# Splitting the scalar steps of a weight conversion, moving one state scaling, and taking two more diagonals from token rows

## The chip, the cores and the metric

The kernel runs on one core of one Trainium2 chip. A core has TensorE (PE, with its weight loads PEld), VectorE (DVE), ScalarE (ACT), GpSimd (POOL), and SyncE (SP), which here issues nearly all DMAs. The metric is the device time of one execution in microseconds. All numbers are microseconds unless ns is written.

## The reference

Two blocks stand one behind the other. The first is a linear attention with decay, for 4 batches, 8 heads, 768 tokens and head size 48:

```python
for t in range(S):
    kt, vt, rt, wt = (k[:, :, t], v[:, :, t], r[:, :, t], w[:, :, t])
    cur = np.einsum('bhd,bhe->bhde', u[None] * kt, vt)
    y[:, :, t] = np.einsum('bhd,bhde->bhe', rt, state + cur)
    state = wt[:, :, :, None] * state + np.einsum('bhd,bhe->bhde', kt, vt)
```

Its output x (4, 768, 384) goes into a mixer over tokens and then over channels:

```python
xt = x.transpose(0, 2, 1)
h = np.maximum(xt @ w_tok1, 0.0) @ w_tok2
u = x + h.transpose(0, 2, 1)
h2 = np.maximum(u @ w_ch1, 0.0) @ w_ch2
return (u + h2).astype(np.float32)
```

The four weights of the mixer arrive as 64-bit floats (their bits are seen as int64), and the kernel makes 32-bit floats of them itself.

## The kernel before

**Attention in units.** The 768 tokens of a batch are three units of 256; twelve units are numbered 0 to 11, and units 3, 4 and 5 belong to batch 1. In a unit the tokens form chunks of 64. A unit runs these steps (function `unit`, listed with a weight for each by `steps`):

- `ends` (L344) and `begins` (L352) are scans of the decay w; `keys` (L349) and `queries` (L355) multiply k and r by them.
- `tokens` and `copied` (L267, L268) transpose k on TensorE and copy it out on ScalarE; `carry` (L283) makes the outer products of keys and values.
- `scaled` (L406) multiplies the state by a chunk's decay on ScalarE in four instructions; `update` (L416) adds the chunk's outer product on VectorE. They alternate, each needing the other.
- `gram` (L239) multiplies keys and queries within a chunk, and `mask` (L393) keeps what lies strictly below the diagonal.
- The diagonal itself needs r·(u·k) of the untouched r and k. There are two ways to it. In one, `own_u` multiplies k by u on ScalarE (four instructions, L249, into a tile called near), `own_gram` makes a second gram on TensorE, and `own_put` (L366) copies its diagonal into place on VectorE. In the other, r and k are also loaded in token rows (`load_near`, one DMA of 768 KB into the single buffer called near), and `products` does two multiplies and a reduction on VectorE (L371, L373, L376); `sums_put` (L381) puts the sums on the diagonal. Units 0 to 5 use the first way, units 6 to 11 the second.
- `before` (L296) and `after` (L310) form y on TensorE, with a small ScalarE copy `seen` (L302) between; `taken` copies y into x on ScalarE in three pieces (L316).

**Mixer.** `hidden` (L459) and `back` (L466) mix tokens; `turn` (L475, copied by L476) transposes the result; `up` (L483) gives z in 128 x 256 pieces, each of three matmuls (six records) into one of two PSUM banks and then evicted by ScalarE (L485); `down` (L493) multiplies z by the second channel weight for the first 256 tokens of batch 0; everywhere else `quarters` does this with seven products of half size (L511), whose sums go into a single-buffered tile `o` through VectorE (L521 to L554) and out by DMA. The first sum of a stage, L521, writes `o`, and so waits for the stores of the stage before. Three sums of blocks of the second channel weight (`weight_sums`, L449), kept in a tile of the conversion called scratch, are factors of the products.

**Conversion.** Each of the twelve conversions takes two pieces of weight, loads 64-bit words (L193) into one of two buffers, spare and scratch, and runs through: exponent bits (VectorE, L196) and power of two (ScalarE, L197), mantissa (VectorE, L200) and sign (ScalarE, L201), sum with the low word (VectorE, L204), product of power and sign (L207) and two products into the weight (L210). The first three convert the token weights, the other nine the channel weights; the latter are numbered 0 to 8 in this text.

**Order.** Each engine's order is fixed by `strict`: what is listed earlier stands earlier on its engine. The first part, batch 0's attention with the first three conversions, is written by hand. After it, `woven` mixes two lists of steps by the weight of each: a step's place in its list is its share of the list's total weight. So batch 1's attention is mixed with batch 0's mixer and the remaining conversions, whose steps weigh 0.1 each (`single`). SP's order is the planner's, which keeps the DMAs' dependencies. In batch 0 the mixer is woven in this order: `turned` with the first two conversions, the first two `up` stages with the next six, `down` with conversion 8 and three of the weight sums, then quarters, the third `up` stage and its quarters.

Of the kernel before, what the change touches and what calls it, by code (L numbers as in the profile page):

```python
# [19 lines left out]
B, H, S, D = 4, 8, 768, 48  # L20
DM = H * D
T = 64
C = S // 128
UC = 2
UB = C // UC
NU = B * UB
# [35 lines left out]
def rwkv6_then_mixer(  # L62
# [18 lines left out]
    pe, dve, act, pool, sp = nc.tensor, nc.vector, nc.scalar, nc.gpsimd, nc.sync  # L81
# [54 lines left out]

    def load_v(i):
        if i < NU:
            vs[i] = vpool.tile([128, UC, DM], f32, name="vt")
            b, j = divmod(i, UB)  # L140
            sp.dma_start(vs[i], v[b, ts(j, UC * 128), :].rearrange("(c p) e -> p c e", p=128))

    def load_near(i):
        if 2 * UB <= i < NU:
            nears[i] = apool.tile([128, UC, 2, DM], f32, name="near", bufs=1)
            sp.dma_start(nears[i], near[i - 2 * UB])

    load_w(0)
    load_rk(0)
# [32 lines left out]
    def convert(pair, raw):  # L182

        d64 = bits64[raw]
        lo, hi = (d64.rearrange("p (n two) -> p n two", two=2)[:, :, j] for j in range(2))
        top = d64.bitcast(u16).rearrange("p (n four) -> p n four", four=4)[:, :, 3]
        m, mf = mantissas, mantissas.bitcast(f32)
        e, power = exponents[:, 0], exponents[:, 1]
        sign, factor = e.bitcast(bf16), power.bitcast(bf16)

        def load():
            for n, (dst, src) in enumerate(pair):
                sp.dma_start(d64[:, ts(n, 2 * PIECE)].rearrange("p (c k) -> p c k", c=dst.shape[1]), src)  # L193

        def take():
            dve.tensor_scalar(e, top, 0x7FF0, None, op0=ALU.bitwise_and)  # L196
            act.activation(power, e, AF.Relu, bias=rebias, scale=8.0)  # L197

        def mantissa():
            dve.tensor_scalar(m, hi, 0xFFFFF, 0x100000, op0=ALU.bitwise_and, op1=ALU.bitwise_or)  # L200
            act.activation(sign, hi.bitcast(i32), AF.Sign)  # L201

        def add():
            dve.scalar_tensor_tensor(mf, lo, 2.0 ** -32, m, op0=ALU.mult, op1=ALU.add)  # L204

        def put():
            dve.tensor_mul(factor, factor, sign)  # L207
            for n, (dst, src) in enumerate(pair):
                x, by = (t[:, ts(n, PIECE)].rearrange("p (c k) -> p c k", c=dst.shape[1]) for t in (mf, factor))
                dve.scalar_tensor_tensor(dst, x, 2.0 ** -20, by, op0=ALU.mult, op1=ALU.mult)  # L210

        return load, take, mantissa, add, put

    def blocks(t, src, c, k):

# [4 lines left out]
    def conversion(*weights, raw):  # L220
        pieces = [e for w in weights for e in blocks(*w)]
        return [convert(pieces[n:n + 2], raw[n // 2 % len(raw)]) for n in range(0, len(pieces), 2)]
# [346 lines left out]
    def steps(i):  # L569

        e = unit(i)
        up, by = e["updates"], e["scaled"]
        by_tokens = i >= 2 * UB
        sums = e["products"] if by_tokens else [lambda: None] * 3
        some = lambda fs, c: [(c, f) for f in fs]
        return [(0.1, lambda: (load_rk(i + 2), load_v(i + 1))), *([] if by_tokens else some(e["own_u"], 0.2)),
                (2.4, e["ends"]), (1.2, e["keys"]), (0.4, e["ranges"][0]), (2.2, e["begins"]), (1.0, e["tokens"]), (0.2, e["copied"][0]),
                *([] if by_tokens else [(1.0, e["own_gram"])]), (0.2, e["copied"][1]), (1.2, e["queries"]), (0.3, by[0]),
                (1.0, sums[0]), (1.0, e["carry"]), (1.0, sums[1]),
                (0.7, up[0]), (0.3, by[1]), (1.4, e["gram"]), (1.0, sums[2]), (0.1, lambda: load_near(i + 1)),  # L580
                (0.7, up[1]), (0.3, by[2]), (1.2, e["mask"]), (0.7, up[2]), (0.3, by[3]),
                (1.3, e["sums_put"] if by_tokens else e["own_put"]), (0.4, e["ranges"][1]), (0.7, up[3]),
                (0.1, lambda: load_w(i + 2)), (1.0, e["before"]), (1.0, e["after"]), *some(e["taken"], 0.3)]

    hiddens, turned, ups, downs = mixing_of(0)
    h = [f for pair in zip(*hiddens) for _, f in pair]
    to_tok = conversion((wtok1, w_tok1, 2, 256), (wtok2, w_tok2, 2, 256), raw=(0, 1))
# [4 lines left out]
    to_tok[1][0]()  # L592

    e0, e1, e2 = (unit(i) for i in range(UB))
    (_, take0, m0, add0, put0), (_, take1, m1, add1, put1), (load2, take2, m2, add2, put2) = to_tok
    in_turn.update({pe.engine: None, dve.engine: None, act.engine: None})
    s0, s1, s2 = (e["updates"] for e in (e0, e1, e2))
    t0, t1, t2 = (e["scaled"] for e in (e0, e1, e2))
    strict(*e0["own_u"], e0["ends"], e0["own_gram"], e0["begins"], e0["keys"], e0["tokens"], *e0["copied"], e0["queries"], lambda: load_w(2),
           e0["gram"], *e1["own_u"], e1["ends"], e0["carry"], *e0["ranges"], e0["mask"], e0["own_put"], e1["own_gram"], s0[0], t0[1],  # L600
           take0, s0[1], t0[2], m0, e1["begins"], s0[2], t0[3], add0, s0[3], e0["before"], put0, load2,
           e1["keys"], e0["after"], *e0["taken"], e1["tokens"], *e1["copied"], e1["queries"], e1["gram"], *e2["own_u"], t1[0],
           e2["ends"], e1["carry"], lambda: load_v(2), e2["begins"], e1["mask"], e2["own_gram"], e1["own_put"], take1, s1[0], t1[1],
           m1, e2["keys"], s1[1], t1[2], e2["tokens"], e2["queries"], s1[2], t1[3], e2["gram"], *e2["copied"], h[0], h[1], add1, s1[3],
           t2[0], e1["before"], e2["mask"], e2["carry"], e1["after"], *e1["taken"], e2["own_put"], put1, s2[0], t2[1],
           h[2], h[3], take2, s2[1], t2[2], m2, *h[4:6], add2, s2[2], t2[3], *h[6:8], s2[3], e2["before"], put2, e2["after"],
           *e2["taken"], lambda: (load_w(3), load_rk(3), load_v(UB), load_w(4), load_rk(4)), to_ch[0][0], to_ch[1][0],
           *e1["ranges"], *h[8:], *e2["ranges"], lambda: sp.dma_start(u_rows, u_all))

    def single(steps, n):  # L610
        return [(0.1, f) for f in steps[n < 2:]]
# [12 lines left out]
    for bt in range(B):  # L624
        ahead = []
        if bt == 0:
            to_ch = [single(e, n) for n, e in enumerate(to_ch)]
            both = [f for e in zip(ups[0], ups[1]) for f in e]
            ahead = woven(turned, sum(to_ch[:2], []))
            of_weights = [(0.1, lambda n=n: weight_sums(n)) for n in range(4)]  # L630
            pieces = woven(both, sum(to_ch[2:8], [])) + woven(downs[0][:6], to_ch[8]) + woven(downs[0][6:], of_weights[:3])
            pieces += downs[1][:4] + of_weights[3:] + downs[1][4:] + ups[2] + downs[2]
        else:
            hiddens, turned, ups, downs = mixing_of(bt)
            pieces = [e for h in hiddens for e in h] + turned
# [112 lines left out]
```

## Time and profile before

| what | us |
|---|---|
| three timed runs: median (lowest to highest) | 563.14 (561.61 to 563.43) |
| the profiled execution: its time | 558.57 |
| the profiled execution: span on the core | 557.0 |
| TensorE busy, ScalarE busy | 514.3, 208.4 |
| own gram of one unit on the chain (L239) | 1.09 |
| products of one unit, three instructions (L371, L373, L376) | 0.952, 0.955, 0.944 |
| one power (L197), one sign (L201) | 1.14, 1.13 |
| four scalings of one state (L406), mean of one | 0.323 |

Busy time of an engine is a sum over the span, and says nothing of what ends the run. The chain of waits follows the work that ended last back to the start; a group's "idle before" names what the engine waited for. In the rows of the stages, busy times of several engines lie beside each other. A row of the timeline gives start, length, engine, line, operation and the tiles that are written and read, and in brackets the idle time before it and its releaser.

### The profile page before, as it was taken

Reading aid. Unit: us, or ns where it says so; the run is one execution under the profiler, and the core shown is the slowest. Engines: PE = TensorE matmul, PEld = TensorE weight load, DVE = VectorE, ACT = ScalarE, POOL = GpSimd, SP = SyncE. Lnnn points to the kernel's source line nnn. Section 1 sums busy time; section 2 is a strip of 40 time slices with the busy share of each in tenths; the row PEclk is TensorE's granted clock in tenths of the full one; section 3 lists DMA queues with packets and bytes.
Section 4 is the critical chain, followed back from the end, with each engine's and each line's share of the span. In section 5 each row is a group of like instructions: output and inputs, shape, how many; then the busy total and the mean of one; then the engine's idle time right before and its main releaser. Section 6 shows DMA issues by size and latency. Waiting matters only on the chain.

```text
span 557.0 us, 12483 instructions
## 1 busy us (share of the span) xinstructions
PE 514.3 (92%) x5526; PEld 436.7 (78%) x5526; DVE 291.9 (52%) x413; ACT 208.4 (37%) x533; POOL 1.3 (0%) x10
## 2 busy tenths in 40 slices
PE   3478899889899999999899999999899999999994
PEld 3465577757789868988889868988888958999994
DVE  7997598983752754282572654292471610313222
ACT  3675876660433234334233234423323213111110
POOL 0000000000000000000000000000000000000000
PEclk9769999999999999999999999999999999999998
DMA  8867546612213212222212302001000000000000
GB/s 314 313 181 233 164 152 209 191 29 97 57 40 114 87 39 86 58 68 86 59 67 86 87 15 82 29 30 58 2 28 2 16 13 1 1 29 2 29 2 32
DMA packets 20653, 44.42 MB, mean 80 GB/s; under 512 B 2097, under 2 KB 12977, under 8 KB 20593
## 3 DMA queue, kind: packets, MB, share of 16 engines
q1 hardware_dynamic: 20448, 43.56, 24.3%
q8 instruction: 45, 0.74, 0.6%
q14 instruction: 16, 0.12, 0.1%
q10 hardware_dynamic: 144, 0.00, 0.0%
HBM read 38.84 MB, written 4.72 MB: 78 GB/s over the span
## 4 chain that ended last, share of the span: by engine, by line
PE 74%; DVE 14%; ACT 4%; DMA 3%; issue 2%; SPq 0%; DVEq 0%; ACTq 0%
PE z_ps L483 29%; PE q_ps L511 22%; PE h_ps L459 5%; PE h_ps L466 4%; PE h_ps L493 3%; PE y_ps L296 3%; DVE to_end L344 3%; PE y_ps L310 3%; PE gram L239 2%; DMA rk<-in_rk_dram 2%; PE kv_ps L283 2%; DVE rk L349 1%; PE gram L267 1%; PE xT_ps L475 1%; ACT scratch L201 1%
## 5 line engine op out<-in xcount | busy, mean ns | idle before, releaser
L483 PE MATMUL z_ps<-xT,wch 128*128 128x256 f32 x864 | 195.5, 383 | 3.7 <-ACT z L485 2.9
L483 PEld LDWEIGHTS z_ps<-xT,wch 128*128 128x128 f32 x864 | 161.3, 190 | 27.0 <-ACT z L485 3.8
L485 ACT ACTIVATE z<-z_ps 128x256 f32<-128x256 f32 x144 | 55.0, 382 | 139.2 <-PE z_ps L483 138.8
L511 PE MATMUL q_ps<-wch,z 128*128 128x192 f32 x528 | 93.4, 329 | 0.5 <-DVE o L533 0.5
L511 PEld LDWEIGHTS q_ps<-wch,z 128*128 128x128 f32 x528 | 86.3, 190 | 2.1 <-DVE o L533 1.1
L511 PE MATMUL q_ps<-scratch,z 128*128 128x192 f32 x396 | 69.1, 328 | 2.2 <-DVE o L529 2.2
L511 PEld LDWEIGHTS q_ps<-scratch,z 128*128 128x128 f32 x396 | 64.7, 190 | 3.2 <-DVE o L529 3.0
L521 DVE TENSOR_TENSOR o<-x,z 128x192 f32<-128x192 f32 x11 | 3.9, 359 | 108.2 <-ACT z L520 104.2
L406 ACT ACTIVATE before<-state,to_end 112x48 f32<-112x48 f32 x176 | 44.1, 323 | 29.1 <-DVE state L416 27.6
L416 DVE TENSOR_TENSOR state<-before,kv_ps 112x192 f32<-112x192 f32 x40 | 14.0, 351 | 48.4 <-ACT before L406 28.2
L459 PE MATMUL h_ps<-x,wtok 128*128 128x384 f32 x96 | 33.8, 505 | 1.7 <-ACT x L316 1.6
L466 PE MATMUL h_ps<-h,wtok 128*128 128x384 f32 x96 | 35.2, 493 | 0.1
L468 DVE TENSOR_TENSOR x<-x,h_ps 128x384 f32<-128x384 f32 x24 | 13.3, 553 | 36.3 <-PE h_ps L466 36.2
L459 PEld LDWEIGHTS h_ps<-x,wtok 128*128 128x128 f32 x96 | 18.4, 196 | 13.8 <-ACT x L316 2.4
L344 DVE TENSOR_TENSOR_SCAN to_end<-w,starts 112x1041 f32<-112x1041 f32 (+1 forms) x13 | 28.1, 2160 | 2.1 <-DMA w<-in_w_dram 1.7
L352 DVE TENSOR_TENSOR_SCAN w<-w,starts 112x1041 f32<-112x1041 f32 x12 | 27.8, 2320 | 0.1
L316 ACT COPY x<-y_ps 64x384 f32<-64x384 f32 (+1 forms) x36 | 17.1, 475 | 20.1 <-PE y_ps L310 19.8
L466 PEld LDWEIGHTS h_ps<-h,wtok 128*128 128x128 f32 x96 | 16.7, 190 | 9.9 <-ACT h L461 2.5
L296 PEld LDWEIGHTS y_ps<-before,rk 48*64 48x64 f32 x704 | 13.6, 140 | 12.6 <-issue 9.9
L296 PE MATMUL y_ps<-before,rk 48*64 48x48 f32 x704 | 15.2, 227 | 8.4 <-DVE state L416 7.7
L336 ACT ACTIVATE junk<-to_end,least 112x1041 uint8<-112x1041 f32 x12 | 13.9, 1162 | 19.7 <-DVE to_end L344 19.7
L239 PE MATMUL gram<-rk,near 48*64 48x64 f32 x384 | 8.9, 252 | 13.4 <-ACT near L249 8.4
(85 smaller groups left out, 481.0 us busy)
## 6 DMA issues: line engine op xcount, KB each, us to landing
rk<-in_rk_dram SPq DMA_DIRECT2D x36, 192.0 KB, 3.9
w<-in_w_dram SPq DMA_DIRECT2D x11, 520.5 KB, 3.7
spare<-in_w_ch_dram SPq DMA_DIRECT2D x10, 512.0 KB, 4.9
vt<-in_v_dram SPq DMA_DIRECT2D x12, 384.0 KB, 4.6
out_dram<-o SPq DMA_DIRECT2D x24, 192.0 KB, 1.9
near<-in_near_dram SPq DMA_DIRECT2D x6, 768.0 KB, 4.3
scratch<-in_w_ch_dram SPq DMA_DIRECT2D x8, 512.0 KB, 4.6
rk<-in_rk_dram SPq DMA_DIRECT2D x6, 512.0 KB, 8.2
```

The costliest lines, as they stand in the source:

```text
L239: fours(lambda q, j, rows, cols: pe.matmul(g[cols, q, ts(ca, T)], k_[rows, ds(ca * 128 + j * T, T)], r_[rows, ds(ca * 128 + j * T, T)], st ...
L296: pe.matmul(y[put(q, j), q, ds((c * A + a) * D, D)], r_[q * P:q * P + D, ds((c * A + a) * 128 + j * T, T)], before[g][q * P:q * P + D, a, ...
L310: pe.matmul(y[put(q, j), q, ts(ca, D)], at[ts(j, T), q, ca, :], vt[ts(j, T), c, ts(2 * a + q, D)], start=False, stop=ca == 0, skip_group_c ...
L316: return [lambda: act.copy(x[:, 0], got[:, 0])] + [lambda n=n: act.copy(x[ts(n, P), 1], got[ts(1 - n, P), 1]) for n in range(2)]
L344: dve.tensor_tensor_scan(to, of, start, 0.0, op0=ALU.mult, op1=ALU.add)
L352: dve.tensor_tensor_scan(w_[:ROWS], w_[:ROWS], starts[:ROWS], 0.0, op0=ALU.mult, op1=ALU.add)
L406: act.mul(t[:ROWS, a], state[bt, g][:ROWS, a], by_last(c, j)[:, a:a + 1])
L459: pe.matmul(sums[i], wtok1[:, c, ts(i, 128)], x_of()[:, c, :], start=(c == 0), stop=(c == C - 1))
L466: pe.matmul(ps, wtok2[:, i, ts(c, 128)], h1[:, i, :], start=(i == 0), stop=(i == DTOK // 128 - 1))
L483: pe.matmul(ps, wch1[:, m, ts(jt, 128)], xT[:, m, ts(s, SEG)], start=(m == 0), stop=(m == DM // 128 - 1))
L485: act.activation(zs[s][:, jt, :], ps, AF.Relu)
L511: pe.matmul(ps, a[:, j, :], b[:, j, :], start=(j == 0), stop=(j == HJ - 1))
```

## The change

Three things are changed.

A conversion's `take` and `mantissa` each held a VectorE and a ScalarE instruction; now each of the four instructions is a step: exponent, mantissa, power (`raise_two`), add, signs, put. In the hand-written part power and sign stand next to where they were for the first two conversions, and behind mantissa and add for the third. In the woven part the steps of a conversion are six and not four, at 0.1 each, so that the places of the other steps shift a little too.

In the hand-written part the three copies of unit 1's y (`e1["taken"]`) stand behind unit 2's first state update and second state scaling instead of ahead of unit 2's `own_put`.

Units 4 and 5 (the fifth and sixth) take their diagonal from token rows as units 6 to 11 do: no `own_u` and no `own_gram`, two more loads of near, and the three products and `sums_put` in place of `own_put`. Unit 3 still uses the second gram.

```diff
     def load_near(i):
-        if 2 * UB <= i < NU:
+        if UB < i < NU:
             nears[i] = apool.tile([128, UC, 2, DM], f32, name="near", bufs=1)
-            sp.dma_start(nears[i], near[i - 2 * UB])
+            sp.dma_start(nears[i], near[i - UB - 1])
...
-        def take():
+        def exponent():
             dve.tensor_scalar(e, top, 0x7FF0, None, op0=ALU.bitwise_and)
+
+        def raise_two():
             act.activation(power, e, AF.Relu, bias=rebias, scale=8.0)
 
         def mantissa():
             dve.tensor_scalar(m, hi, 0xFFFFF, 0x100000, op0=ALU.bitwise_and, op1=ALU.bitwise_or)
+
+        def signs():
             act.activation(sign, hi.bitcast(i32), AF.Sign)
...
-        return load, take, mantissa, add, put
+        return load, exponent, mantissa, raise_two, add, signs, put
...
-        by_tokens = i >= 2 * UB
+        by_tokens = i > UB
...
-    (_, take0, m0, add0, put0), (_, take1, m1, add1, put1), (load2, take2, m2, add2, put2) = to_tok
+    (_, x0, m0, p0, add0, g0, put0), (_, x1, m1, p1, add1, g1, put1), (load2, x2, m2, p2, add2, g2, put2) = to_tok
...
-           take0, s0[1], t0[2], m0, e1["begins"], s0[2], t0[3], add0, s0[3], e0["before"], put0, load2,
+           x0, p0, s0[1], t0[2], m0, g0, e1["begins"], s0[2], t0[3], add0, s0[3], e0["before"], put0, load2,
...
-           t2[0], e1["before"], e2["mask"], e2["carry"], e1["after"], *e1["taken"], e2["own_put"], put1, s2[0], t2[1],
-           h[2], h[3], take2, s2[1], t2[2], m2, *h[4:6], add2, s2[2], t2[3], *h[6:8], s2[3], e2["before"], put2, e2["after"],
+           t2[0], e1["before"], e2["mask"], e2["carry"], e1["after"], e2["own_put"], put1, s2[0], t2[1],
+           *e1["taken"], h[2], h[3], x2, s2[1], t2[2], m2, p2, *h[4:6], add2, g2, s2[2], t2[3], *h[6:8], s2[3], e2["before"], put2, e2["after"],
...
-    r, k = (inputs[n].transpose(0, 2, 1, 3).reshape(B, S, DM)[2:].reshape(NU - 2 * UB, UC, 128, DM) for n in ("r", "k"))
+    r, k = (inputs[n].transpose(0, 2, 1, 3).reshape(B, S, DM)[1:].reshape(NU - UB, UC, 128, DM)[1:] for n in ("r", "k"))
```

More of the change, by code (lines that the diff above doesn't have):

```diff
@@ L600, in rwkv6_then_mixer @@
            e0["gram"], *e1["own_u"], e1["ends"], e0["carry"], *e0["ranges"], e0["mask"], e0["own_put"], e1["own_gram"], s0[0], t0[1],
-           take0, s0[1], t0[2], m0, e1["begins"], s0[2], t0[3], add0, s0[3], e0["before"], put0, load2,
+           x0, p0, s0[1], t0[2], m0, g0, e1["begins"], s0[2], t0[3], add0, s0[3], e0["before"], put0, load2,
            e1["keys"], e0["after"], *e0["taken"], e1["tokens"], *e1["copied"], e1["queries"], e1["gram"], *e2["own_u"], t1[0],
-           e2["ends"], e1["carry"], lambda: load_v(2), e2["begins"], e1["mask"], e2["own_gram"], e1["own_put"], take1, s1[0], t1[1],
-           m1, e2["keys"], s1[1], t1[2], e2["tokens"], e2["queries"], s1[2], t1[3], e2["gram"], *e2["copied"], h[0], h[1], add1, s1[3],
-           t2[0], e1["before"], e2["mask"], e2["carry"], e1["after"], *e1["taken"], e2["own_put"], put1, s2[0], t2[1],
-           h[2], h[3], take2, s2[1], t2[2], m2, *h[4:6], add2, s2[2], t2[3], *h[6:8], s2[3], e2["before"], put2, e2["after"],
+           e2["ends"], e1["carry"], lambda: load_v(2), e2["begins"], e1["mask"], e2["own_gram"], e1["own_put"], x1, p1, s1[0], t1[1],
+           m1, g1, e2["keys"], s1[1], t1[2], e2["tokens"], e2["queries"], s1[2], t1[3], e2["gram"], *e2["copied"], h[0], h[1], add1, s1[3],
+           t2[0], e1["before"], e2["mask"], e2["carry"], e1["after"], e2["own_put"], put1, s2[0], t2[1],
+           *e1["taken"], h[2], h[3], x2, s2[1], t2[2], m2, p2, *h[4:6], add2, g2, s2[2], t2[3], *h[6:8], s2[3], e2["before"], put2, e2["after"],
            *e2["taken"], lambda: (load_w(3), load_rk(3), load_v(UB), load_w(4), load_rk(4)), to_ch[0][0], to_ch[1][0],
```

## The prediction

> **What bounds the kernel now.** Times are of the one profiled execution (span 557.0, its own time 558.57; the three timed runs have a median of 563.14). I read the shares and slices first, then busy time by stage, then the waits and the order of time in the stages that the change touches.
>
> ```profile
> PE 514.3 (92%) x5526; PEld 436.7 (78%) x5526; DVE 291.9 (52%) x413; ACT 208.4 (37%) x533; POOL 1.3 (0%) x10
> ...
> PE   3478899889899999999899999999899999999994
> ...
> DVE  7997598983752754282572654292471610313222
> ```
>
> TensorE carries the whole, but not everywhere: in the first eight slices (to 111 us) VectorE is as full. By stage (columns: length; busy time and instructions of PE, PEld, DVE, ACT, POOL; clock, DMA share, GB/s):
>
> ```profile
> 60.00:90.00 30.00, 28.03 (x244) 20.85 (x243) 28.18 (x38) 20.76 (x37) 0.00 (x0) 1.00 0.42 140
> 90.00:105.00 15.00, 12.90 (x117) 10.81 (x118) 13.19 (x19) 11.12 (x28) 0.00 (x0) 1.00 0.67 205
> 105.00:120.00 15.00, 13.52 (x155) 9.72 (x154) 13.71 (x17) 11.67 (x23) 0.00 (x0) 1.00 0.47 125
> 120.00:135.00 15.00, 15.00 (x234) 9.70 (x232) 9.39 (x11) 2.98 (x10) 0.00 (x0) 1.00 0.14 50
> 135.00:150.00 15.00, 12.50 (x192) 11.76 (x189) 9.83 (x16) 3.65 (x12) 0.00 (x0) 1.00 0.15 45
> 150.00:165.00 15.00, 15.00 (x144) 13.61 (x138) 7.20 (x8) 7.90 (x18) 0.00 (x0) 1.00 0.25 76
> ```
>
> Stage Z (71 to 115, the first two `up` stages beside unit 3 and conversions 2 to 8): PE has 24 z groups of 1.29 and 6.3 of unit 3, some 37.3 us in 43.4, so 6 us are lost. The waits of 70 to 116 and the order at its end say to what:
>
> ```profile
> ACT scratch L197 <- DVE scratch L196: 7.0, 3, 3.0
> ...
> PE z_ps L483 <- ACT z L485: 2.9, 3, 1.5
> DVE scratch L207 <- ACT scratch L201: 2.7, 3, 1.1
> ...
> PE h_ps L493 <- ACT z L485: 1.5, 1, 1.5
> ```
>
> ```profile
> 112.13 1.13 ACT L201 ACTIVATE scratch<-scratch 128x1024 bf16<-128x1024 int32 x1
> 113.16 1.29 ACT L249 ACTIVATE near<-rk,u_col 112x256 f32<-112x256 f32 x3
> ...
> 114.36 0.36 ACT L485 ACTIVATE z<-z_ps 128x256 f32<-128x256 f32 x1
> ...
> 114.77 5.43 PE L493 MATMUL h_ps<-wch,z 128*128 128x384 f32 x16 [1.48 <-ACT z L485]
> ```
>
> ScalarE stands at the power of a conversion (L197) until VectorE gives the exponent, and z evictions queue behind it; PE has two z banks and stops. At the end, z waits behind a sign (L201) and three `own_u` multiplies (L249), and `down` (h_ps L493) starts late. From 115 PE is full up to a transfer, then VectorE carries the chain:
>
> ```profile
> 122.37 1.09 PE gram L239 x64
> ...
> 135.02 3.83 DMA out_dram<-o
> ...
> 164.11 1.09 PE gram L239 x64
> ```
>
> The two grams are the `own_gram` of units 4 and 5, both on the chain; the transfer is the second row block of `o`, whose single buffer the next stage's first sum (L521) overwrites. From 150 PE is full.
>
> **What the Trainium skill says.** "Perfetto Trace Analysis", section Sequencer Loop: an engine's instructions are queued and wait for their semaphores there; the ACT lines above agree (z at 114.36 although its matmuls ended near 111.7). "DMA: Bandwidth & Descriptors", Anatomy of one DMA: a semaphore wait is made by the issuing sequencer; agreed, SP's four rk issues at 135.47 take 13.97. Same page, Queues, rings and completion order: each DMA engine consumes a ring in order, and the completion write lands only after all earlier writes of that engine. The trace shows one effect near this: the first `o` block lands in 1.9, the second, with two rk loads behind it, in 3.8.
>
> **The change part by part.** I carry the new order of each engine through this trace's spacings (ACT power or sign 1.05, z 0.28, four scalings 0.92; DVE exponent or mantissa 0.60, add 1.14, put 1.21, mask 1.15).
>
> *Scaling ahead of the copies of y (unit 2's second scaling).* Before it starts at 48.54, behind unit 1's copies (47.07 to 48.52), and VectorE waits 2.45 for it. Now it starts at 46.55, when its state is there, and the copies run 47.5 to 48.9. Behind the copies `h[4:6]` slips 0.4 (48.56 to 48.96) but the across matmuls that follow wait for the fourth scaling anyway. That scaling comes after power and sign, at 51.95 instead of 52.42. Gain 0.45, carried by the chain through unit 2, h and the first `back`.
>
> *Power and sign later, 61 to 71.* VectorE's order is unchanged there. A copy of xT now passes ahead of the waiting power (turn 2's at 66 instead of 69.03), so the 0.25 and 0.87 that PE waits go, but turn 5 needs VectorE's last x sum, behind an add: first z at 70.7 for 71.23. With the 0.45 inside, 0.5.
>
> *The same in stage Z.* Mantissa now directly follows exponent, so scans, keys and one state sum move behind it by 0.6 each; a z passes ahead of each power. VectorE is the bound: its fifth exponent comes at 93.2 (93.83 before). Then a loss: the third state sum of unit 3 now stands behind exponent and mantissa 6 (101.35 for 100.66), the scaling that needs it holds ScalarE until 101.7, and two z wait behind it. Product 7 on VectorE is at 113.45 for 113.29: the gain is eaten. But the last z are no longer behind the sign (1.05) or behind four `own_u` (4 x 0.43 = 1.7, L249, gone): the last z of the first half is evicted at 112.0 to 112.3, its matmuls ended 110.5, and `down` starts at 112.35 for 114.77. Gain 2.4.
>
> *Diagonal of unit 4.* Its own gram (1.09) goes; its products (952, 955 and 944 ns by L371, L373, L376: 2.85) fall at 125.4 to 128.5 and behind the second `o`, where VectorE idled 2.6, 2.3 and 4.0 us; if that cover fails, up to 2.85. The masked copy costs the same (1307 for 1302 ns). Conversion 8 ends 1.2 later in VectorE's order, because queries now precede its product: 124.15, while PE wants it at 125.2. `down` is 48 records in 16.2 (16 take 5.4), kT 0.87, kv 1.08 and gram 1.09: with 0.1 of bank wait the quarter products start at 131.7 for 134.98. Gain 3.3.
>
> *Its transfer.* near (768 KB, 4.3 to landing) is issued near 86, wanted at 125: hidden. SP is also reordered: half of conversion 8's load stands behind vt of unit 5, issued 108.4 instead of 105.5. The loads of that place (`spare` at 105) took 3.9 to 7.8, so it lands 112.3 to 116.2, wanted 115.35: 0 to 0.9, taken as 0 since conversion 8 has 1.05 of slack on PE.
>
> *The `o` transfer.* Last `o` sum: gram now precedes it, so it starts at 131.75 for 134.45, 2.7 earlier. Between the two `o` stores SP now has two rk loads, behind the second follows near of unit 5. Bounds of landing: 1.9 (first block) and 9.7 (two rk of 3.9 in series and 1.9). I take 3.83 as before, since two rk loads are beside it in both. From L521 to the freed bank the VectorE row is as long as before (5.6). So 2.7 survive of 3.3.
>
> *Diagonal of unit 5.* Own gram 1.09 goes, from a stretch where PE is full. The reduce and the earlier mask stand ahead of evictions of the quarter products: counted from the first product's start, p4 is evicted by 2.95 and wanted at 3.9; p2 by 5.8 and wanted at 5.9. No stall, by 0.1. From 200 on the order is unchanged.
>
> Sum: 2.7 + 1.09 = 3.8, less 0.1 for that thin slack: 3.7. 558.57 becomes 554.9; the median stands 4.57 above the profiled execution, so 563.14 - 3.7 = **559.4**.
>
> **The rivals.**
> *A. The second `o` lands fast (1.9).* For: rk is ahead of it by over 1 us instead of 0.45 behind. Against: near follows it. L521 then starts at 134.3, and p6 at 140.25 for 144.58: 4.3 + 1.09 = 5.4, 557.7.
> *B. Stage Z gives nothing.* The late third state sum holds ScalarE, and through z the PE; for it speaks that DVE is 94% full there. `down` then starts where it did, 114.8; the second `o` sum then starts at 133.95 for 134.45 (0.5), and unit 5's gram is left (1.09): 1.6, 561.5.
> *C. Slower: the second `o` waits for the rk pair in series.* Place: L521 behind its store. Price: landing 9.7 instead of 3.83, 5.9 lost, 2.2 slower, 565.3. It decides from a landing of 7.5. Against: 384 KB at the 332 GB/s seen at 88 to 92 is 1.2.
> *D. It doesn't do what it says*: excluded; the built order has both grams gone and the steps apart.
>
> **How the numbers follow.** Chances: forecast 0.56, A 0.20, B 0.14, C 0.10. About 0.3% (1.7 us) can be told from no change: faster 0.76 (forecast and A), same 0.14 (B), slower 0.10 (C). Range: A with a little more, 557.2, to B with conversion 8's 0.9 late, 562.6; C is left out, and some of A's end.
>
> **What would show it.** `down` starting near 112.4; quarter products near 131.7; L521's wait for its store near 4; no own gram after unit 3; z rows from 200 on earlier by 3.7. Wrong if `down` starts at 114 or later (B), if L521 starts after 138 (C), or if VectorE's first exponent of conversion 8 waits for a DMA over 2 us.

## The result, and the profile after

| runs | median, us | lowest to highest | runs |
|---|---|---|---|
| before, beside the changed kernel | 563.25 | 559.49 to 564.71 | 7 |
| changed | 557.02 | 556.37 to 557.32 | 7 |
| changed again, beside the last two experiments | 556.17 | 554.7 to 557.35 | 6 |

The ratio is 0.9897, with a 95% interval of 0.9872 to 0.9922: 5.8 us faster by the ratio, where 3.7 were forecast. The profiled executions say less: 557.02 with a span of 555.3, against 558.57 and 557.0, so only 1.5. The two views don't contradict each other. The 143 timed executions of the kernel before that ran beside the experiments lie between 558.38 and 565.51, so its profiled one, 558.57, is among the very fastest; the section on the clock shows what they differ in.

Behind L193 the lines of the changed kernel stand up to four higher (z_ps L483 is now L487, its eviction L489, `o` L521 is L525, state L416 is L420, a sign L201 is L205). The changed kernel's shares and its slices of the granted clock:

```profile
PE 514.6 (93%) x5398; PEld 437.0 (79%) x5398; DVE 296.8 (53%) x419; ACT 205.7 (37%) x525; POOL 1.3 (0%) x10
...
PEclk9668999899999999999999999999999999999998
```

Two grams are gone from TensorE (5526 to 5398 records, 128 fewer), six instructions are new on VectorE (three products for each of two units). TensorE is busy as long as before, 514.6 for 514.3, although 2.2 of gram are gone: the digit 8 in the eighth slice says that some of its work ran slower. By stage (columns as before: length, busy time of PE, PEld, DVE, ACT, POOL, clock, DMA share, GB/s):

```profile
105.00:120.00 15.00, 13.82 (x150) 10.19 (x151) 10.81 (x16) 9.34 (x18) 0.00 (x0) 0.89 0.42 123
120.00:135.00 15.00, 15.00 (x175) 9.63 (x174) 13.87 (x16) 4.50 (x12) 0.00 (x0) 1.00 0.15 51
```

VectorE's work has moved from the first of these rows (13.71 to 10.81) into the second (9.39 to 13.87); two of unit 4's three products, 0.95 each, are in it, at 128.50 and 130.63. The clock of the first row is 0.89, which was 1.00. The waits of 70 to 116 and the timeline show why:

```profile
ACT scratch L199 <- DVE scratch L196: 3.5, 2, 1.9
...
PE y_ps L300 <- DVE state L420: 2.4, 1, 2.4
```

```profile
101.21 0.69 DVE L196 TENSOR_SCALAR scratch<-spare 128x1024 uint16<-128x1024 uint16 x1
101.81 0.69 DVE L202 TENSOR_SCALAR scratch<-spare 128x1024 uint32<-128x1024 uint32 x1
102.41 0.35 DVE L420 TENSOR_TENSOR state<-before,kv_ps 112x192 f32<-112x192 f32 x1
...
105.48 1.14 PE L300 MATMUL y_ps<-before,rk 48*64 48x48 f32 x48 [2.39 <-DVE state L420]
...
106.55 2.55 PE L487 MATMUL z_ps<-xT,wch 128*128 128x256 f32 x6
...
109.02 1.75 PE L314 MATMUL y_ps<-vt,at 64*64 64x48 f32 x64
...
115.55 1.88 PE L497 MATMUL h_ps<-wch,z 128*128 128x384 f32 x5 [0.69 <-ACT z L489]
```

ScalarE no longer stands 7.0 for exponents, and no z eviction makes TensorE wait 2.9. In their place is one wait of 2.39: TensorE has done the z groups ahead of y by 103.09 and y can start only at 105.48. Unit 3's third state sum (102.41) stands behind the exponent and mantissa of conversion 6, and y behind the scaling and the fourth sum that follow it. After it the z group (six records) takes 2.55, which is 1.56 elsewhere, and the within-y, TensorE's second part of y, 1.75 for 1.15; the part that waited is called across-y below. These 1.6 are lost to the clock, and `down` begins at 115.55, later than the 114.77 of before, not at 112.35.

From there the chain of the profiled execution is:

```profile
132.16 1.09 PE gram L243 x64
...
135.36 2.77 DMA out_dram<-o
```

The one gram left there is unit 4's ordinary one; its own gram is gone. The second `o` landed in 2.77 (3.83 before).

### The profile page after: what moved, and what is told of

The parts are those of the page before. It is cut to its first block, busy times and chain, and to the rows that moved or that the text cites. A ratio compares the mean times of both kernels' runs of the same rounds, so it can differ in the third digit from the quotient of the medians.

```text
span 555.3 us, 12227 instructions
## 1 busy us (share of the span) xinstructions
PE 514.6 (93%) x5398; PEld 437.0 (79%) x5398; DVE 296.8 (53%) x419; ACT 205.7 (37%) x525; POOL 1.3 (0%) x10
## 4 chain that ended last, share of the span: by engine, by line
PE 74%; DVE 14%; ACT 5%; DMA 3%; issue 2%; SPq 0%; DVEq 0%; ACTq 0%
PE z_ps L487 29%; PE q_ps L515 22%; PE h_ps L463 5%; PE h_ps L470 4%; PE h_ps L497 3%; PE y_ps L300 3%; DVE to_end L348 3%; PE y_ps L314 2%; DMA rk<-in_rk_dram 2%; PE gram L243 2%; PE kv_ps L287 2%; PE gram L271 1%; ACT before L410 1%; PE xT_ps L479 1%; DVE rk L353 1%
## 5 line engine op out<-in xcount | busy, mean ns | idle before, releaser
L487 PE MATMUL z_ps<-xT,wch 128*128 128x256 f32 x864 | 196.1, 383 | 0.9 <-DVE o L553 0.9
L487 PEld LDWEIGHTS z_ps<-xT,wch 128*128 128x128 f32 x864 | 161.7, 190 | 24.3 <-DVE o L553 1.7
L489 ACT ACTIVATE z<-z_ps 128x256 f32<-128x256 f32 x144 | 55.2, 383 | 143.9 <-PE z_ps L487 143.4
L525 DVE TENSOR_TENSOR o<-x,z 128x192 f32<-128x192 f32 x11 | 3.9, 358 | 108.9 <-ACT z L524 106.8
L420 DVE TENSOR_TENSOR state<-before,kv_ps 112x192 f32<-112x192 f32 x40 | 14.1, 352 | 44.8 <-ACT before L410 26.4
L480 ACT COPY xT<-xT_ps 128x384 f32<-128x384 f32 x24 | 11.5, 477 | 25.1 <-PE xT_ps L479 25.1
```

Source lines behind the costliest of these rows:

```text
L420: dve.tensor_add(new[:ROWS], L["before"][g][:ROWS], got)
L487: pe.matmul(ps, wch1[:, m, ts(jt, 128)], xT[:, m, ts(s, SEG)], start=(m == 0), stop=(m == DM // 128 - 1))
L489: act.activation(zs[s][:, jt, :], ps, AF.Relu)
```

## The clock: what single executions differ in

The trace records the granted clock of TensorE, which is half or full in stretches that are multiples of 3.41 us; one such length is called a window here. Every profiled execution runs at half clock through most of 18 to 46, where TensorE is sparsely used, and at its end. Between them they differ:

| profiled execution | span | half clock between 48 and 540 |
|---|---|---|
| before | 557.0 | none |
| before, again | 562.9 | 55.58 to 62.4, 274.03 to 277.44 |
| changed | 555.3 | 106.98 to 110.39 |
| changed, again | 553.0 | 105.62 to 109.04 |
| diagonals alone | 557.0 | 148.39 to 151.8 |
| split alone | 564.6 | 54.6 to 61.42, 150.17 to 153.58, 276.46 to 279.88 |
| scaling alone | 556.4 | none |
| diagonals and scaling | 555.2 | 146.7 to 150.11 |
| split at weight 0, alone | 561.6 | 54.91 to 61.74, 273.36 to 276.78 |
| all three, split at weight 0 | 557.8 | 56.52 to 59.94, 397.86 to 401.27 |
| unit 5's diagonal alone | 559.3 | 56.32 to 63.15, 151.89 to 155.31 |
| diagonals and scaling, y behind | 553.1 | none |

The Trainium skill, "TensorE: Matmul & The Clock Gate", Part 1, section What's actually happening, describes this: a window of 3413 ns that runs freely, so that its phase against the kernel differs from run to run, and half rate after an idle window. The traces agree on the length and the phase. Its section Why this matters for your kernels puts the danger at gaps over about 3 us; here less was enough. The stretches of one window ahead of and in such a drop (columns as in the table by stage), first of the changed kernel, then of diagonals and scaling:

```profile
103.56:106.98 3.42, 1.50 (x50) 1.45 (x51) 2.56 (x5) 3.42 (x6) 0.00 (x0) 1.00 0.00 0
106.98:110.39 3.41, 3.41 (x58) 2.50 (x60) 3.38 (x5) 0.99 (x5) 0.00 (x0) 0.50 0.90 253
```

```profile
143.28:146.70 3.42, 1.62 (x68) 1.37 (x67) 2.50 (x6) 0.55 (x3) 0.00 (x0) 1.00 0.02 5
146.70:150.11 3.41, 3.41 (x12) 3.12 (x10) 0.00 (x0) 0.02 (x1) 0.00 (x0) 0.50 0.35 115
```

TensorE was busy for 1.50 and 1.62 of 3.42, with single waits of 2.39 and 1.80. No sharp threshold comes out. In the run with all three parts and the split at weight 0, a window with a busy share of 0.46 (104.31 to 107.72) was followed by full clock. In the kernel before, run again, one with a share of 0.73 (52.16 to 55.58, in it the small matmuls of y, 64 x 48) was followed by half clock. The same program's first profile has a window with the same share and the same y (50.62 to 54.04), and full clock behind it.

The late stretch at 274 shows the same more plainly. In both profiles of the kernel before, a y of the third batch waits 1.59 for its state:

```profile
269.22 1.15 PE L296 MATMUL y_ps<-before,rk 48*64 48x48 f32 x64 [1.59 <-DVE state L416]
```

```profile
272.96 1.15 PE L296 MATMUL y_ps<-before,rk 48*64 48x48 f32 x64 [1.59 <-DVE state L416]
274.04 3.88 PE L511 MATMUL q_ps<-wch,z 128*128 128x192 f32 x12
```

In the first profile the product behind it takes 2.22, in the second 3.88. So one and the same wait in one and the same program cost a half-clock window in one execution and none in the other. That the position of the wait in the windows decides it is likely, and no run here shows it.

How much it costs over all runs can be read from the runs themselves, since each has its mean granted clock. One window at half clock lowers the mean by 3.413 x 0.5 / 557 = 0.0031. A common straight line through the 276 runs of all kernels gives 1.01 us (0.91 to 1.11) for each such step. With it the kernels can be compared at one clock (0.975). That is a fit, not an experiment: it mixes windows that cost 1.7 with early ones that cost less, and lines through the runs of each kernel alone have slopes from 0.3 to 1.4. A comparison "at one clock" also takes out what a change does to the clock itself. The changed kernel's first runs are compared with the 62 runs of before, since their own runs of before have no clock on record.

| kernel | ratio to before, 95% interval | mean clock | difference to before at one clock, us |
|---|---|---|---|
| before (62, 32 and 27 runs) | | 0.9725, 0.9729, 0.9723 | |
| changed | 0.9897 [0.9872, 0.9922] | 0.9734 | -4.7 ± 0.8 |
| changed, again | 0.9903 [0.9868, 0.9938] | 0.9772 | -4.4 ± 0.8 |
| diagonals alone | 0.9951 [0.9933, 0.9969] | 0.9709 | -3.2 ± 0.5 |
| split alone | 1.0072 [1.0042, 1.0102] | 0.9693 | +3.5 ± 0.7 |
| scaling alone | 0.9966 [0.9950, 0.9981] | 0.9764 | -0.9 ± 0.5 |
| diagonals and scaling | 0.9926 [0.9897, 0.9955] | 0.9736 | -4.4 ± 0.8 |
| all three, split at weight 0 | 0.9925 [0.9898, 0.9953] | 0.9787 | -2.2 ± 0.7 |
| split at weight 0, alone | 1.0021 [1.0004, 1.0037] | 0.9715 | +0.7 ± 0.5 |
| unit 5's diagonal alone | 0.9978 [0.9960, 0.9996] | 0.9709 | -1.8 ± 0.5 |
| diagonals and scaling, y behind | 0.9877 [0.9839, 0.9915] | 0.9763 | -5.9 ± 0.8 |

## The experiments

### Before again, and each part alone

The kernel before, unchanged, ran as a run of its own beside the three parts.

> The kernel before, unchanged, as a yardstick. Two theories of why the timed gain (1.03%, some 5.8 us) is larger than the 1.5 us between the two profiled executions. P (path): the row lengths are the same in every execution and the first profile of before was simply an early one of a spread; this profile then shows the same stage borders to 0.3 us after the first 30 us, and its time lies within 1 us of the first profiled 558.6. C (clock): in executions of before at 562 and above the TensorE clock is lowered in a stretch after 60 us in which the first profile of before showed 1.00; if this profile's time is 562 or more, its slices after 60 us then show a clock below 1.00 somewhere and the matmul rows there are longer by some 2 to 5 us in sum, and the stages after 200 us are of equal length.

561.98 median, ratio 0.999 [0.9972, 1.0008]. Its profiled execution took 564.5 and has the half-clock stretch of 55.58 to 62.4, which the first lacks. The window before it has unit 2's y in two pieces with a wait of 0.67 between, and the next token matmuls take 5.14 where they took 2.85. From there up to 139 everything is 3.25 later, of which 0.76 was there at 46; from 139, behind an `o` transfer of 4.30 (3.83 in the first profile), 3.7; and behind the half-clock window at 274, 5.4. Theory C was right that half-clock stretches make the difference, but not that the stages after 200 are of equal length. So 563 is no fixed distance above 558.6: the same program has executions with and without such stretches.

**Diagonals alone**:

```diff
-        if 2 * UB <= i < NU:
+        if UB < i < NU:
...
-        by_tokens = i >= 2 * UB
+        by_tokens = i > UB
```

The near loads and the layout of what they load are changed along with it, as in the change itself.

> Only the diagonals of units 4 and 5 come from token rows; steps and scaling as before. My step sum (P): down starts 1.3 to 1.7 earlier relative to the rows around it, because four own_u leave the queue ahead of the last z; with two own grams of 1.09 the whole is 2.5 to 3.9 faster, ratio 0.993 to 0.9955. Rival (steps carry it): only the two grams, 2.2, ratio 0.996. If C holds, the ratio is 0.99 and the run lists a higher mean clock than before_again.

559.21 median, ratio 0.9951; 3.2 at one clock. The mean clock was not higher than before's (0.9709 for 0.9725), so the gain comes from work that left the path. In its profile the first z to `down` takes 42.22 for 43.43 in the first profile of before, and `down` to the quarter products 18.82 for 20.21. Unit 5's stretch, from the first z behind to the next batch's token matmuls, takes 35.17 for 36.67. In between, 2.6 are lost again: unit 4's across-y stands one product earlier than before, waits for its state, and a half-clock window follows. That shift is a side effect of the weave, too. A unit with token rows has no `own_u` (four steps of 0.2) and no `own_gram` (1.0) in its list, so its other steps change their places.

**Split alone**:

```diff
-        return load, take, mantissa, add, put
+        return load, exponent, mantissa, raise_two, add, signs, put
```

> Only the splitting of power and sign into later steps; diagonals and scaling as before. P: at most 0.5 by the xT copies that pass ahead, and down 1.05 earlier since the last z of the first half stands ahead of the last sign, less the late third state sum: 0.5 to 1.5 faster, ratio 0.997 to 0.999. Rival: the state sum behind exponent and mantissa holds ScalarE and PE, and it is up to 1 slower, ratio 1.002. C: the longer PE gap of about 2.4 us at 102 to 105 lowers the clock right behind it, and the z and y rows there take 1.5 to 1.7 times their length, as in the profile after.

566.27 median, ratio 1.0072: 4 slower, where P had it faster and the rival at most 1 slower. The clock drop of theory C came, but at 150 and not behind 105. The timeline shows where:

```profile
149.21 0.35 DVE L420 TENSOR_TENSOR state<-before,kv_ps 112x192 f32<-112x192 f32 x1
...
149.70 1.61 PE L300 MATMUL y_ps<-before,rk 48*64 48x48 f32 x64 [4.44 <-DVE state L420]
151.24 3.35 PE L515 MATMUL q_ps<-scratch,z 128*128 128x192 f32 x12
```

The two added steps of each conversion shift everything that is woven with them. Unit 4's across-y now stands ahead of a quarter product that used to precede it. That y needs a state which VectorE has only at 149.5, so TensorE stands 4.44, and the clock drops: the product takes 3.35 for 2.22.

**Scaling alone**:

```diff
-           t2[0], e1["before"], e2["mask"], e2["carry"], e1["after"], *e1["taken"], e2["own_put"], put1, s2[0], t2[1],
-           h[2], h[3], take2, s2[1], t2[2], m2, *h[4:6], add2, s2[2], t2[3], *h[6:8], s2[3], e2["before"], put2, e2["after"],
+           t2[0], e1["before"], e2["mask"], e2["carry"], e1["after"], e2["own_put"], put1, s2[0], t2[1],
+           *e1["taken"], h[2], h[3], take2, s2[1], t2[2], m2, *h[4:6], add2, s2[2], t2[3], *h[6:8], s2[3], e2["before"], put2, e2["after"],
```

> Only the copies of unit 1's y behind unit 2's second scaling. P: fourth scaling 0.9 to 1.4 earlier (power and sign stay where they were, so that scaling is ahead of them no more than before): 0.3 to 0.5 faster, ratio 0.999. Rival: PE runs at about half clock there in the profile of after (0.50 from 40 to 45), so TensorE and not the scaling ends that stage, and nothing is gained, ratio 1.000.

559.74 median, ratio 0.9966; 0.9 ± 0.5 at one clock. About half of its 1.9 is the clock's (0.9764 for 0.9725, 1.3 windows), half the path's. The timeline of unit 2, first of this kernel, then of before:

```profile
45.77 0.35 DVE L416 TENSOR_TENSOR state<-before,kv_ps 112x192 f32<-112x192 f32 x1
...
51.34 1.54 PE L296 MATMUL y_ps<-before,rk 48*64 48x48 f32 x64
51.51 1.00 ACT L406 ACTIVATE before<-state,to_end 112x48 f32<-112x48 f32 x4
...
55.86 1.56 PE L459 MATMUL h_ps<-x,wtok 128*128 128x384 f32 x4 [1.57 <-ACT x L316]
```

```profile
46.17 0.35 DVE L416 TENSOR_TENSOR state<-before,kv_ps 112x192 f32<-112x192 f32 x1 [0.43 <-PE kv_ps L283]
...
52.42 1.01 ACT L406 ACTIVATE before<-state,to_end 112x48 f32<-112x48 f32 x4
```

The fourth scaling starts at 51.51 (52.42 before), y runs in one piece and no longer waits in the middle, and the token matmuls behind it start at 55.86 for 56.77: 0.91. But 0.40 of that stood there before the moved scaling could act: unit 2's first state sum starts at 45.77 for 46.17, behind a half-clock stretch that ended at 42.96 and not at 43.80. From that sum to the fourth scaling it is 5.74 for 6.25: the move is worth 0.51. The unchanged kernel's second profile has 6.26, and the two kernels with this part and without the split have 5.72.

The three parts together give -3.2 + 3.5 - 0.9 = -0.6, where the change gives -4.7. They don't add up, and the split is the part that behaves otherwise when it is alone. The next runs ask why.

### The split among the other parts

**Diagonals and scaling, no split** (the edits of the two kernels above together):

> The diagonals of units 4 and 5 from token rows and the fourth scaling ahead of the copies of y, without the power and the sign as steps of their own. Parts theory: the gains of the two parts add, because they lie in different stages; alone they gave 2.7 and 1.9 (3.2 and 1.0 once runs of the same mean granted clock are compared), so this kernel stands 4 to 4.6 under the kernel before, ratio near 0.992, and what the changed kernel has beyond that (it stood 5.8 to 6.3 under) comes from the two further steps. Clock theory: the two parts change only which half-clock windows occur, so the mean granted clock of this kernel's runs is higher than before's 0.9725 and at the same clock the gain is under 2. In its profile the across-y of unit 4 stands ahead of the last but one product of the first batch's third quarter, as in the kernel with the diagonals alone, and waits there 1.5 to 2 for VectorE's state.

557.37 median, ratio 0.9926; 4.4 at one clock, clock 0.9736. The parts theory holds: -3.2 and -0.9 add, and the mean clock is 0.2 windows above that of before on the same chip, too little for the clock theory. Its first z starts at 71.32, as in the first profile of before (71.34), so the two can be laid side by side: `down` 113.52 for 114.77 (1.25 earlier), the quarter products 132.34 for 134.98 (2.64), the product that follows the wait for `o` 141.29 for 144.58 (3.29). That first z is no later than before's although the scaling is moved, because unit 2's first state sum was 0.53 late here (46.70). Then

```profile
145.31 1.15 PE L296 MATMUL y_ps<-before,rk 48*64 48x48 f32 x64 [1.80 <-DVE state L416]
146.39 3.90 PE L511 MATMUL q_ps<-wch,z 128*128 128x192 f32 x12
```

y waits for VectorE's state, the clock drops, and 12 records take 3.90 for 2.22. Of 3.29 only 0.65 are left at the first z behind (153.35 for 154.00).

**The changed kernel with the split's steps at weight 0 in the weave**:

```diff
-        return [(0.1, f) for f in steps[n < 2:]]
+        weights = [0.1, 0.1, 0.1, 0.0, 0.1, 0.0, 0.1]
+        return list(zip(weights, steps))[n < 2:]
```

> The changed kernel with the power and the sign still steps of their own, but with weight 0 in the weave instead of 0.1, so that TensorE's and VectorE's order is that of the two other parts without the split (ScalarE's power and sign alone stay later). Weave theory: the split acts through the two extra weights, which shift everything woven with it, so this kernel equals the one without the split within 1, near ratio 0.992. Lateness theory: the split acts by letting ScalarE do other work before a power or a sign that VectorE has not fed yet, so this kernel equals the changed one, near ratio 0.989, and its third state sum of unit 3 is no longer behind the exponent and mantissa of conversion 6, which is worth up to 1.9 more.

557.31 median, ratio 0.9925 [0.9898, 0.9953], as without the split and as the weave theory said; the interval does not exclude the 0.989 of the lateness theory. But its clock was higher, 0.9787, and at one clock it is 2.2 ± 0.9 behind the kernel without the split. The profile, which is its slowest execution, shows a way for that. TensorE's and VectorE's order is the same in the two kernels, and only ScalarE's differs; VectorE waited 7.8 in five waits for signs (60 to 140), the longest 5.47, against 3.4 in three without the split, and TensorE then waited for the weight of the conversion behind that sign:

```profile
116.03 0.69 DVE L211 TENSOR_TENSOR scratch<-scratch 128x1024 bf16<-128x1024 bf16 x1 [5.47 <-ACT scratch L205]
...
128.35 1.56 PE L497 MATMUL h_ps<-wch,z 128*128 128x384 f32 x4 [1.50 <-DVE wch L214]
```

From `down` to the quarter products it takes 21.49, against 18.82 without the split. So a later sign can cost, in this execution; by the plain ratios the two kernels can't be told apart.

**The split alone, at weight 0** (the same edit on the split alone):

> The split alone, with weight 0 for the two added steps, so that TensorE's and VectorE's order is that of the kernel before. With weight 0.1 the split alone was 4.3 slower. Weave theory: that loss came from the shifted order (the across-y of unit 4 one product earlier, TensorE idle for 4.44 ahead of it); here it is gone, the time is within 1 of before (ratio 0.998 to 1.001), and the wait ahead of the across-y is again near 0.65. Lateness theory: a later power and sign make the factor late for VectorE; then it stays 2 to 4 slower, with VectorE waiting for ScalarE ahead of the factor's product.

562.78 median, ratio 1.0021 [1.0004, 1.0037]. With before's order restored, 2.8 of the split's 3.5 (at one clock) are gone, and the across-y waits 0.66 again. So the larger part of that loss was the shifted order. The rest, 0.7 ± 0.5, fits lateness, without being shown to be it; the waits of 60 to 140 have

```profile
DVE scratch L211 <- ACT scratch L205: 6.4, 5, 2.7
```

where the kernel before has 2.7 in three. This row grows by more than the time does.

### The whole again, the y put behind, unit 5 alone

**Changed, again**, on the same chip as the next two:

> The changed kernel again, beside the two others on one chip. It was 1.0% under the kernel before in its first seven runs and the kernel without the split 0.7% under. Parts theory: the diagonals and the scaling carry all of the gain, and the split nothing, so here the changed kernel is 4 to 5 under before (ratio 0.991 to 0.993) and within 1 of the kernel without the split. Rival: the split is worth the difference, then it is 5.5 to 6.5 under (ratio 0.988 to 0.990).

556.17 median, ratio 0.9903; 4.4 at one clock. That is the same as diagonals and scaling without the split. So the split brings 0 ± 1 here; whether it is worth a fraction of a microsecond can't be told from these runs. It gives and takes: it shifts the order so that unit 4's y waits 0.66 and not 1.80, and no drop follows there, but it puts the third state sum late, where both profiles of the changed kernel have the drop.

**Diagonals and scaling, unit 4's across-y one product later**:

```diff
-                (0.1, lambda: load_w(i + 2)), (1.0, e["before"]), (1.0, e["after"]), *some(e["taken"], 0.3)]
+                (0.1, lambda: load_w(i + 2)), *([(1.0, lambda: None), (1.0, lambda: (e["before"](), e["after"]()))] if i == UB + 1 else [(1.0, e["before"]), (1.0, e["after"])]), *some(e["taken"], 0.3)]
```

> The diagonals and the scaling without the split, and unit 4's across-y moved one product later, directly ahead of its within-y. In the profile without this move TensorE stood 1.80 for VectorE's state ahead of that y and then ran a 3.41 window at half clock, which cost some 1.7. Path theory: the wait shrinks from 1.80 to under 0.7 and the work after it is 1.1 earlier, ratio near 0.990. Clock theory: with the wait the half-clock window goes too in those runs that have it, so that it gains 1.1 to 2.8 and the mean granted clock rises above 0.9736. Rival: VectorE's subtraction and sums of that quarter, which need the product now done first anyway, set the time; then nothing changes, ratio near 0.9926.

554.95 median (553.07 to 556.6), ratio 0.9877 [0.9839, 0.9915], the best of all; 5.9 at one clock. The stretch has

```profile
144.58 2.22 PE L511 MATMUL q_ps<-wch,z 128*128 128x192 f32 x12 [0.57 <-DVE o L533]
146.72 1.15 PE L296 MATMUL y_ps<-before,rk 48*64 48x48 f32 x64
148.20 1.15 PE L310 MATMUL y_ps<-vt,at 64*64 64x48 f32 x64 [0.33 <-ACT seen L302]
```

and the window that was 47% busy is filled, at full clock:

```profile
144.69:148.10 3.41, 3.18 (x76) 2.83 (x76) 2.50 (x6) 0.11 (x1) 0.00 (x0) 1.00 0.02 5
```

The wait of 1.80 is gone, and with it the half-clock window. The path theory gave 0.990; the gain over the same kernel without the move is 2.4 by the medians of two chips, 1.5 ± 1 at one clock, so both theories' terms seem to be in it. In the profiles the stretch from that product to the first z behind takes 9.56, against 12.06 without the move. Its interval overlaps that of the changed kernel, so that it beats it is likely and not settled.

**Unit 5's diagonal alone**:

```diff
-        if 2 * UB <= i < NU:
+        if UB + 1 < i < NU:
...
-        by_tokens = i >= 2 * UB
+        by_tokens = i > UB + 1
```

> The kernel before with only unit 5's diagonal from token rows; unit 4 keeps its own gram. The prediction's sum gave unit 5 its own gram alone, 1.1, and unit 4 the rest, 2.2 to 2.8. By the profiles the stretch of unit 5 gained 1.5. So 1.1 to 1.5 under before, ratio 0.9973 to 0.9980. Rival: unit 4's gain is given back at the first batch's end, where VectorE sets the pace, and unit 5 carries most of it; then 2.5 to 3 under, ratio near 0.995.

560.77 median, ratio 0.9978 [0.9960, 0.9996]: 1.2, as expected, 1.8 at one clock. So unit 4's diagonal adds about 1.5 to it (2.7 less 1.2, on two chips). But 1.2 is not the worth of unit 5's diagonal by itself. With unit 5's four `own_u` and its `own_gram` out of the list, unit 4's across-y stands one product earlier here too, although unit 4 is unchanged: it waits 2.44, and the product behind it runs at half clock, 3.90 for 2.22. Where that loss is absent, as with y put behind, unit 5's stretch still gains its 1.5.

## Why the prediction was right, and where it was not

The forecast was 559.4 with a range of 557.2 to 562.6. The ratio puts the changed kernel at 557.3 for the 563.14 of before (563.14 x 0.9897), inside the range at its low end; the gain is 5.8 where the sum was 3.7. The direction was right, and so were most of the causes. But the largest term, stage Z, gave nothing, and the prediction's own signs say so: `down` began at 115.55 and 114.00 in the two profiles of the changed kernel, where 114 or later was named as wrong (rival B); and the sum L521 (now L525) started at 138.32 in one of them, where after 138 was named as wrong (rival C), in the other at 136.45.

The gains by stage, against the first profile of before, each stage from the one starting point to the next, and the first of them not before unit 2, so that what the early half clock shifts drops out:

| stage | forecast | changed | changed, again |
|---|---|---|---|
| unit 2's first state sum to the first z | 0.5 | 0.42 | 0.40 |
| first z to `down` (stage Z) | 1.9 | -0.19 | -0.14 |
| `down` to the quarter products | 0.9 | 1.19 | 1.18 |
| quarter products to the first z behind | -0.6 | 0.23 | 0.56 |
| that z to the next batch's token matmuls | 1.0 | 1.50 | 1.50 |
| sum | 3.7 | 3.15 | 3.50 |

So a sum near the forecast came out by luck: the 2 that stage Z did not give came back in part from the `o` transfer, which was forecast to cost 0.6, and from the two units. The terms one by one:

- **Scaling ahead of the copies**: 0.45 predicted; from unit 2's first state sum to the fourth scaling it is 5.87 in both profiles of the changed kernel, for 6.25: 0.38. Without the split it is 0.51 to 0.53. This term was right.
- **Steps in 61 to 71**: first z at 70.7 was predicted. The changed kernel's two profiles have 71.93 and 70.43, and the difference lies before 48, in how long the early stretches at half clock are. From unit 2's first state sum it is 24.75 and 24.77 (25.17 before): 0.4, which is the scaling's. With the scaling alone it is 24.66, so the split gave nothing here.
- **Stage Z**: predicted was `down` at 112.35. It began at 115.55 and 114.00. The loss that the prediction named came true: the third state sum behind exponent and mantissa 6. It was priced as two z held on ScalarE; what TensorE met was a wait of 2.39 for the state (2.37 in the other profile) and then a half-clock window of 1.6. From first z to `down` it is 43.6 in both profiles (43.43 before); taking the 1.6 off gives an estimate of 42.0, so about 1.4 of the predicted 1.9 net would have been there. The kernels with the diagonals and without the split, which have no such window there, take 42.2. Product 7 on VectorE was put at 113.45 and came at 116.53, behind its later sign; TensorE had no wait for it.
- **Unit 4's own gram**: 1.19 and 1.18 gained; 0.9 was in the sum (3.3 less 2.4). The products were hidden beside PE, and so were the near load and conversion 8's half load, which landed at 116.1, near the late end of the bound, with its exponent at 118.47.
- **The second `o`**: 3.83 taken, 2.77 and 2.45 measured, between forecast and rival A. Its bounds held. Why it was shorter is not shown: over the twelve profiles it took from 2.01 to 4.30, all of that range with the two stores next to each other as before; the split alone, with two rk loads between them like the changed kernel, has 3.76. Rival C, the rk pair in series ahead of it, was not seen; the start at 138.32 comes from the late `down`.
- **Unit 5's own gram**: 1.09 predicted; 1.5 by the profiles (from the first z behind, 0.64 earlier, to the token matmuls of the next batch, 188.53 for 190.67). Of the rest, 0.33 is the wait for `seen`, which is gone because a product now stands between the two halves of y.
- **The split**: the sum had its late third state sum as a loss, and the sign's 1.05 in the 2.4 as a gain. Within the change it brings 0 ± 1. It is not harmless: alone it costs 4, and that depends on which step of the weave ends up ahead of which product, which the prediction didn't ask of unit 4's y.

The fit gives a gain of 4.4 to 4.7 at one clock. The stages above add up to 3.15 and 3.50, each with one half-clock window of 1.6 in stage Z, so that an estimate without that window is 4.75 and 5.1. What is left to 5.8 is the clock: the changed kernel's mean clock was 0.3 to 1.6 windows higher than that of before, and the profile that the prediction started from is an execution of before without a half-clock window between 48 and 540, while its second profile has three. How much of the 5.8 each carries is not measured.

The step that failed is the price of stage Z: 1.9 net was forecast and -0.1 to -0.2 measured. The prediction put the late third state sum down as z held up on ScalarE, carried waits as lost time alone, and never asked which of them would slow what comes after; the runs show a TensorE wait of 2.39 and a half-clock window of 1.6 in its place.

Open stays which pattern of use makes the clock drop, what the second `o` waits for, and what the split alone is worth within the change. A kernel with unit 4's y behind and an earlier third state sum together with the split was not tried.

## What to carry to other kernels

Price a wait of TensorE twice: the wait itself, and 1.7 us for a window at half clock if that stretch ends up about half empty, as something that may or may not come in a single execution. The cheapest gain here was moving one y behind a ready product. Before subtracting two traces, set them on the same starting point: here the early stretches alone moved unit 2's first state sum between 45.59 and 47.28. In a weave by weights, adding steps of "no cost", or taking steps out, moves everything else: look at which instruction now stands ahead of which on TensorE before pricing the steps themselves. And test the parts alone and in pairs: one of these three is a loss alone and neutral with the others.

## What was not expected of the hardware

- The clock drops after windows whose longest wait is 1.8 or 2.4 us, not only after idle ones: 0.47 and 0.44 of the window busy in the two shown above. Between shares of 0.46 and 0.73 both full and half clock followed, in one case behind the same wait of 1.59 in the same program.
- One window at half clock costs 1.6 to 1.7 where TensorE carries the chain (2.55 and 1.75 for 1.56 and 1.15 in one; 3.90 for 2.22 in another).
- A store of 192 KB, the second of the first stage that writes `o`, took 2.01 to 4.30 over the twelve profiles, with loads around it; most of the later stores took 1.9.
